# A retention and gated feed-forward kernel: the first two pair tiles taken from two batches in place of one

## The chip, the cores and the metric

The kernel runs on one core of a Trainium2 chip. The metric is the device time of one execution, in microseconds. The core has a matrix engine (TensorE, PE in the profile, with its weight loads as PEld), a vector engine (VectorE, DVE), a scalar engine (ScalarE, ACT), a general engine (GpSimd, POOL), an engine that issues transfers (SyncE, SP), and 16 DMA engines. Each engine works through its own instructions in order, and waits on semaphores for what other engines make.

## The reference

```python
B, H, S, D = 8, 8, 576, 64
scores = q @ k^T / sqrt(D)                       # per batch and head
gamma  = 1 - 2 ** (-5 - arange(H))
Dmat   = where(i >= j, gamma_h ** (i - j), 0)
attn   = (scores * Dmat) @ v                     # no softmax
x      = attn.transpose(0, 2, 1, 3).reshape(4608, 512)
gate   = sigmoid(x @ w_gate)                     # w_gate, w_val: 512 x 1536
out    = ((gate * (x @ w_val)) @ w_out)          # w_out: 1536 x 512
```

Inputs and output are float32. Since the decay is a product of a factor of the query's place and one of the key's, what a chunk of tokens owes to all earlier ones is q times a state, and the state is the sum of the outer products of k and v over those earlier tokens.

## The kernel before

**Tokens.** The 4608 columns of x are dealt out in an order of their own. The first 768 are three "pair tiles" of 256 tokens, listed in `PAIRS` (line 105) as (batch, which 256 tokens): the first 512 tokens of batch 0, then the first 256 tokens of batch 1. The rest goes in steps of 128 tokens (`STEPS`); the first two steps are chunks 2 and 3 of batch 1. Half a pair tile, called a = 0 or 1, is a chunk of 128 tokens with a place r = 0 or 1 inside each pair of neighbours.

**A pair tile.** q and k are cast to bfloat16 with their decay factors (`cast_pair`), turned on TensorE (`turn`, tiles kT and qT, copied by ACT), multiplied to scores (`pair_qk`, tiles qkp) and masked on DVE to ptp. Line 586 (`pair_intra`, for the third tile line 549 in `third_intra`) multiplies ptp with the values vp. The chunk's part from earlier chunks is line 596 (`pair_inter`), q times a state. The sum in tile pvp is copied to xT by ACT or DVE (`pair_out`, line 606).

**States before.** `first_st` (line 508) makes the outer products of the first two tiles into two PSUM banks, `tile_sv` and `first_sum` cast or add their useful quarters into `sbd`, three states in a row: after chunk 0, 1 and 2, and `sbd[3]` after all of batch 0's first 512 tokens. The third tile's state comes from `pair_st` (line 492). It needs for its second chunk only the state of its own first chunk (`third_inter`, into a bank `apart` that `third_out` adds). `first_batch_state` puts batch 0's last state in its final layout with two transfers and two copies on ACT.

**The hidden layer of the first 512 columns** is made in 12 blocks of 128 hidden units, each with a gate (hg, sigmoid on ACT) and a value (hv, multiplied on DVE into gv). Blocks 0 and 1 are made on 256 columns at a time by `h_half` (line 1344), the first half of them between the steps of the second tile; blocks 2 to 11 by `h_both` (line 1280) on 512 columns. Then `op_first` (line 1430) multiplies gv with w_out into three banks, op_0 to op_2, and later a fourth; the third tile's steps stand between these matmuls.

**What sets the order.** The order is written out by hand in the main body; every engine keeps the order of these calls. The weights come by the queue of SP in the order of the `load_w`, `load_wo` and `load_pair` calls, are cast by POOL, ACT or DVE as each `cast_w` or `cast_wo` names it, and a landing buffer is used again after its cast. `fill` puts idle matmuls on TensorE. `w_sums` makes sums of weight quarters on DVE for the later blocks (line 365; tiles wgt and wvt). Everything from the 768th column on is set by tables that the change leaves alone.

Of the kernel before, what the change touches and what calls it, by code (L numbers as in the profile page):

```python
# [16 lines left out]
def kernel(  # L17
# [19 lines left out]
    nc = tc.nc  # L37
# [67 lines left out]
    PAIRS = [(0, 0), (0, 1), (1, 0)]  # L105
# [107 lines left out]
    load_w(2, 2)  # L213
    load_w(4, 4)
    load_w(8, 4)
    pair_2 = load_pair(2)
    for n_wo, n_pair in ((2, 4), (4, 2), (6, 0)):
        for _ in range(n_wo):
            load_wo(sum(1 for x in parts if x[0] == "o"))
        for _ in range(n_pair):  # L220
            next(pair_2)
# [60 lines left out]
    sbd = [lead.tile([P, M, P], BF16, name="sbd0")]  # L282
    sbd += [sum_tile([P, 2, M, P], BF16, f"sbd{i}", SUMS - i)[:, 0] for i in range(1, 4)]
# [201 lines left out]
    def pair_st(A, a):  # L485
        b, a2 = PAIRS[A]
        if b not in st_tiles:
            st_tiles[b] = st_psum.tile([P, M, D], FP32, tag="st", name=f"st_{b}")
        for r in range(2):
            for m in range(M):  # L490
                for hh in range(2):
                    nc.tensor.matmul(st_tiles[b][half(hh), m, :], lhsT=natural["k", A][half(a), r, 2 * m + hh, :],
                                     rhs=natural["v", A][half(a), r, head(A, m, hh), :],
                                     start=(a2 == 0 and a == 0 and r == 0 and m == 0),
                                     stop=(a2 == 1 - b and a == 1 and r == 1 and m == M - 1),
                                     skip_group_check=True)

    def first_st(*tiles):


        for A, a in tiles:
            if (0, A) not in st_tiles:
                pool, tag = ((st_psum, "st"), (ffn_psum, "ffn"))[A]
                st_tiles[0, A] = pool.tile([P, M, P], FP32, tag=tag, name=f"st_0_{A}")
        for m in range(M):
            for r in range(2):
                for A, a in tiles:
                    nc.tensor.matmul(st_tiles[0, A][:, m, :],
                                     lhsT=natural["k", A][half(a), r, 2 * m:2 * m + 2, :],
                                     rhs=natural["v", A][half(a), r, 2 * m:2 * m + 2, :],  # L510
                                     start=(a == 0 and r == 0 and m == 0), stop=(a == 1 and r == 1 and m == M - 1),
                                     skip_group_check=True)

    def first_sum(sb, name, copy):

        share = nat_pool.tile([P, M, D], FP32, tag="s32", name=name, bufs=5)
        for hh in range(2):
            copy(out=share[half(hh)], in_=st_tiles[0, 1][half(hh), :, half(hh)])
        for hh in range(2):
            nc.vector.tensor_tensor(out=sb[half(hh), :, half(hh)], in0=st_tiles[0, 0][half(hh), :, half(hh)],  # L520
                                    in1=share[half(hh)], op=ALU.add)

    def tile_sv(A, a, engs):
        b, a2 = PAIRS[A]
        sb = sbd[2 * A + a]
        for hh in range(2):
            engs[hh](out=sb[half(hh), :, half(hh)], in_=st_tiles[b, 0][half(hh), :, half(hh)])
        state[b, 2 * a2 + a, 1] = sb
# [27 lines left out]
    def third_inter(bank):  # L556

        apart = bank[0].tile([P, 2, P], FP32, tag=bank[1], name="pvp_5_apart")
        for u in range(2):
            for y in range(2):  # L560
                for x in range(2):
                    nc.tensor.matmul(pair_ps[5][2 + u][0][half(x), 2 + u, :] if y else apart[half(x), u, :],
                                     lhsT=state[1, 0, 1][half(y), 2 * u + x, :],
                                     rhs=turned["qp", 2][half(y), 2 * u + x, P:2 * P],
                                     start=(y == 0 and u == 0), stop=(u == 1), skip_group_check=True)
        return apart

    def third_out(apart):

        ps = pair_ps[5][0][0]  # L570
        share = sum_tile([P, 2, 256], FP32, "apart", 4)[:, :, 0:P]
        nc.vector.tensor_copy(out=share, in_=apart)
        cols = slice(5 * P, 6 * P)
        nc.vector.tensor_tensor(out=x_out(slice(0, 2), cols), in0=x_in(ps[:, 0:2], cols), in1=x_in(share, cols), op=ALU.add)
        nc.scalar.copy(out=x_out(slice(2, 4), cols), in_=x_in(ps[:, 2:4], cols))
# [15 lines left out]
    def pair_inter(A, a):  # L591
        b, a2 = PAIRS[A]
        c = 2 * a2 + a
        for m in range(M):
            ps, at_m, of = pair_ps[2 * A + a][m]
            nc.tensor.matmul(ps[:, at_m, :], lhsT=state[b, c - 1, 1][:, m, :],
                             rhs=turned["qp", A][:, m, a * P:(a + 1) * P],
# [173 lines left out]

    def first_batch_state():

        whole = new_state((0, LAST - 1, NJ - 1))
# [520 lines left out]
    for A in range(2):  # L1295
        for g in range(2):
            cast_pair("v", A, g, on_pool)
# [267 lines left out]
```

## Time and profile before

| what | value |
|---|---|
| runs | 304.59, 305.26, 305.45 us |
| median | 305.26 us |
| span of the profiled execution | 304.6 us (the page gives no other time for it) |
| instructions | 10848 |
| granted TensorE clock, mean | 0.994 |
| HBM traffic | 37.75 MB read, 9.44 MB written |

Times in the profile's lists count from the span's start. A row of a timeline gives the start, the length and the engine and line, then the tile written and what it reads, the shape, and in brackets how long the engine sat idle ahead of it and on what. The chain of waits is followed back from the last instruction: at each step to what released it. A row of the windows gives one stretch: its length, then for each engine the busy time and number of instructions, then the granted clock, the busy share of the DMA engines and the GB/s they moved. TensorE's ends are modelled, and a few per cent of its records are missing.

### The profile page before, as it was taken

How to read it: one execution, taken by the hardware profiler on the slowest of the kernel's cores; microseconds unless marked ns; L12 is line 12 of the kernel's file. 1: busy time of each engine (PE TensorE's matmuls, PEld its weight loads, DVE VectorE, ACT ScalarE, POOL GpSimd, SP SyncE). 2: the span in 40 equal slices, each digit the busy share in tenths (PEclk: the TensorE clock that was granted, in tenths of full speed). 3: DMA queues.
4: the chain of work that ended last, by engine and by line, in shares of the span. 5: the costliest groups of instructions: out<-in, count | busy, mean ns of one | idle time of the engine just before them, and what ended most of it. 6: DMA issues, size and time to landing. Idle time of an engine off the chain costs nothing.

```text
span 304.6 us, 10848 instructions
## 1 busy us (share of the span) xinstructions
PE 296.0 (97%) x4427; PEld 244.8 (80%) x4436; DVE 244.7 (80%) x476; ACT 196.8 (65%) x420; POOL 208.6 (68%) x255
## 2 busy tenths in 40 slices
PE   8799999999999999999999999999999999999994
PEld 7674455877858888888888888888888888888883
DVE  6847997887997898689978997898789968946793
ACT  6646563526549656975796579657965886648640
POOL 5675653654557699769976997699769916751670
PEclk9989999999999999999999999999999999999999
DMA  7999999999999993999499919994980390012004
GB/s 214 328 346 399 360 296 230 186 215 199 204 209 238 194 240 82 242 264 213 110 210 234 213 44 219 225 203 52 214 199 2 100 245 9 2 56 87 1 2 138
DMA packets 144994, 55.01 MB, mean 181 GB/s; under 512 B 124336, under 2 KB 136880, under 8 KB 144944
## 3 DMA queue, kind: packets, MB, share of 16 engines
q1 hardware_dynamic: 144144, 53.66, 73.5%
q8 instruction: 35, 0.57, 0.8%
q10 hardware_dynamic: 800, 0.66, 0.7%
q14 instruction: 15, 0.12, 0.1%
HBM read 37.75 MB, written 9.44 MB: 155 GB/s over the span
## 4 chain that ended last, share of the span: by engine, by line
PE 92%; DMA 2%; SPq 2%; DVE 1%; issue 1%; POOL 0%
PE gatea L974 12%; PE wa L974 12%; PE qa L1088 11%; PE qe L1088 9%; PE gatee L974 6%; PE we L974 6%; PE h_v L850 4%; PE h_g L850 3%; PE op L1430 3%; PE op L1190 3%; PE gateg L974 3%; PE wg L974 3%; PE hv L1280 3%; PE hg L1280 3%; PE val L680 2%; DMA v32p<-in_v_dram 2%
## 5 line engine op out<-in xcount | busy, mean ns | idle before, releaser
L425 POOL TENSOR_TENSOR qk<-k,ktab 128x512 bf16<-128x512 f32 x30 | 32.4, 1080 | 11.8 <-DMA k<-in_k_dram 10.9
L1088 PEld LDWEIGHTS <-gsum 128*128 128x128 bf16 x336 | 31.9, 98 | 5.0 <-DVE gsum L911 0.8
L911 POOL TENSOR_TENSOR gsum<-gv 128x256 bf16<-128x256 bf16 (+1 forms) x35 | 26.5, 767 | 13.1 <-DVE gv L999 12.0
L974 PEld LDWEIGHTS <-wg_sb 128*128 128x128 bf16 x308 | 30.1, 98 | 3.7
L425 POOL TENSOR_TENSOR qk<-q,qtab 128x512 bf16<-128x512 f32 x28 | 30.8, 1100 | 3.3 <-DMA q<-in_q_dram 3.3
L974 PEld LDWEIGHTS <-wv_sb 128*128 128x128 bf16 x308 | 30.1, 98 | 3.5
L974 PEld LDWEIGHTS <-wvt 128*128 128x128 bf16 x280 | 27.4, 98 | 3.2
L974 PEld LDWEIGHTS <-wgt_sb 128*128 128x128 bf16 x252 | 24.7, 98 | 2.8
L999 POOL TENSOR_TENSOR gv<-gv,wu 128x512 bf16<-128x512 bf16 x7 | 8.1, 1161 | 25.6 <-DVE wu L1025 25.6
L1088 PEld LDWEIGHTS <-gv 128*128 128x128 bf16 x240 | 23.0, 98 | 3.0
L911 POOL TENSOR_TENSOR gsum<-gv,gsum 128x256 bf16<-128x256 bf16 x37 | 25.4, 715 | 0.0
L669 DVE TENSOR_TENSOR pt<-row,tri 128x256 bf16<-128x256 f32 x60 | 21.3, 414 | 4.4 <-PE row L662 3.7
L740 ACT CAST xT<-val 128x256 bf16<-128x256 f32 x60 | 18.9, 388 | 6.2 <-PE val L695 6.2
L974 PE MATMUL wa<-xsum,wv_sb 128*128 128x256 bf16 x140 | 21.0, 273 | 0.0
L631 ACT CAST sb<-s 128x256 bf16<-128x256 f32 x46 | 17.8, 417 | 3.7 <-DVE s L767 2.5
L974 PE MATMUL gatea<-xsum,wg_sb 128*128 128x256 bf16 x140 | 19.9, 273 | 0.0
L430 POOL CAST v<-v 128x512 bf16<-128x512 f32 x20 | 13.6, 681 | 8.7 <-DMA v<-in_v_dram 8.7
L999 POOL TENSOR_TENSOR gv<-gv,ws 128x512 bf16<-128x512 bf16 x15 | 17.4, 1163 | 2.8 <-DVE ws L1028 2.8
L1028 DVE TENSOR_TENSOR gs<-gatea,gs 128x512 f32<-128x512 f32 x21 | 13.9, 688 | 6.1 <-PE gatea L974 5.2
L1020 DVE TENSOR_TENSOR gatee<-gatea,gs 128x512 f32<-128x512 f32 x14 | 9.8, 700 | 10.0 <-PE gatea L974 7.2
L1028 DVE TENSOR_TENSOR ws<-wa,ws 128x512 f32<-128x512 f32 x21 | 14.4, 686 | 4.1 <-PE wa L974 4.1
L997 ACT ACTIVATE gv<-gs 128x512 bf16<-128x512 f32 x21 | 13.0, 631 | 7.0 <-DVE gs L1028 7.0
(181 smaller groups left out, 858.4 us busy)
## 6 DMA issues: line engine op xcount, KB each, us to landing
k<-in_k_dram SPq DMA_DIRECT2D x26, 256.0 KB, 4.5
q<-in_q_dram SPq DMA_DIRECT2D x26, 256.0 KB, 4.5
v<-in_v_dram SPq DMA_DIRECT2D x26, 256.0 KB, 4.2
out_dram<-ob SPq DMA_DIRECT2D x25, 256.0 KB, 3.2
wg<-in_moe_w_gate_dram SPq DMA_DIRECT2D x12, 256.0 KB, 5.3
wv<-in_moe_w_val_dram SPq DMA_DIRECT2D x12, 256.0 KB, 5.2
wo<-in_moe_w_out_dram SPq DMA_DIRECT2D x12, 256.0 KB, 5.1
v32p<-in_v_dram SPq DMA_DIRECT2D x6, 256.0 KB, 5.2
```

The lines of the kernel that those rows point to most:

```text
L425: eng.tensor_tensor(out=natural_qk[s][:, i].rearrange("p m (y d) -> p y m d", y=2), in0=by_halves(loaded[s][1 - i]), in1=tab, op=ALU.mult)
L430: eng(out=natural["v", s], in_=loaded[s][2])
L631: eng(out=state[key], in_=src)
L669: nc.vector.tensor_tensor(out=probs[s][:, y], in0=row_ps[s][y][:, 0], in1=tri.unsqueeze(1).to_broadcast([P, M, 64]), op=ALU.mult)
L740: nc.scalar.copy(out=x_out(ALL, cols_of(s, i)), in_=x_in(val_ps[s][i], cols_of(s, i)))
L850: nc.tensor.matmul(ps[:, i], lhsT=w_sb[:, kc, (fc + i) * P:(fc + i + 1) * P], rhs=xT(kc, slice(t0, t0 + n)), start=(kc == 0), stop=(kc == ...
L911: eng.tensor_tensor(out=to, in0=a, in1=b, op=op)
L974: nc.tensor.matmul(ps[:, f], lhsT=w[:, kc, f * P:(f + 1) * P], rhs=x[:, kc], start=(first and f == 0 and kc == 0), stop=(f == 1 and kc == ...
L999: eng.tensor_tensor(out=to, in0=to, in1=src, op=ALU.mult)
L1028: nc.vector.tensor_tensor(out=me["s5"], in0=a, in1=me["s5"], op=ALU.add)
L1088: nc.tensor.matmul(ps[:, b], lhsT=left(fp)[:, b * P:(b + 1) * P], rhs=right(fp), start=(first and fp == 0 and b == 0), stop=(fp == NFC // ...
L1280: nc.tensor.matmul(ps, lhsT=(wg_sb if what == "g" else wv_sb)[:, kc, fc * P:(fc + 1) * P], rhs=xT(kc, slice(0, 4 * P)), start=(kc == 0), s ...
```

## The change

`PAIRS` becomes tokens 0 to 255 of batch 0, tokens 0 to 255 of batch 1, tokens 256 to 511 of batch 0. So the first two tiles need only a state of their own first chunk each, and the third tile needs two states of the first batch. What goes with it:

- `first_st` makes the state of a tile's first chunk in two parts, one for each half of the heads; `first_state` casts it. `sbd` has two tiles in place of four. `first_sum`, `tile_sv`, `third_out` and `first_batch_state` go away.
- `pair_st` can take all 128 rows. It runs once for each of the first two tiles, between blocks 0 and 1, and gives the state after 256 tokens (`first`, and in bfloat16 `first_bf`). For the third tile it runs once for each half, in two banks. DVE adds the first half's state to `first`, ACT casts the sum, and `third_inter` multiplies q with both states, in two calls with a marker each.
- Blocks 0 and 1 are made on 512 columns by `h_one`, blocks 2 to 7 two at a time by `h_two`, half of the inner dimension at a time.
- The weights of blocks 4 to 7 are loaded 256 columns at a time; six tiles of w_out come ahead of the third tile's q and k in place of two. More of the value casts are ACT's. 16 idle matmuls fewer are put in.

```diff
-    PAIRS = [(0, 0), (0, 1), (1, 0)]
+    PAIRS = [(0, 0), (1, 0), (0, 1)]
...
-    load_w(2, 2)
-    load_w(4, 4)
+    for f in range(2, 8, 2):
+        load_w(f, 2)
...
-    for n_wo, n_pair in ((2, 4), (4, 2), (6, 0)):
+    for n_wo, n_pair in ((6, 4), (2, 2), (4, 0)):
...
+    def pair_st(A, a, bank):
+        rows_ = slice(0, P) if a is None else half(a)
+        st_tiles[A, a] = bank[0].tile([P, M, D], FP32, tag=bank[1], name=f"st_{A}_{a}")
...
+    def first_st(A, g, bank=None):
+        if g == 0:
+            st_tiles[A] = bank[0].tile([P, M, P], FP32, tag=bank[1], name=f"st_{A}")
+        for m in range(2 * g, 2 * g + 2):
+            for r in range(2):
+                nc.tensor.matmul(st_tiles[A][:, m, :], lhsT=natural["k", A][half(0), r, 2 * m:2 * m + 2, :],
+                                 rhs=natural["v", A][half(0), r, 2 * m:2 * m + 2, :],
+                                 start=(m == 0 and r == 0), stop=(m == M - 1 and r == 1), skip_group_check=True)
+
+    def first_state(A, engs):
+        for hh in range(2):
+            engs[hh](out=sbd[A][half(hh), :, half(hh)], in_=st_tiles[A][half(hh), :, half(hh)])
...
+    def third_inter(same):
+        for u in range(2):
+            for x in range(2):
+                for a in range(2):
+                    y = a if same else 1 - a
+                    kc = 2 * y + u
+                    nc.tensor.matmul(pair_ps[4 + a][kc][0][half(x), kc, :],
+                                     lhsT=state[0, 1 + a, 1][half(y), 2 * u + x, :],
+                                     rhs=turned["qp", 2][half(y), 2 * u + x, a * P:(a + 1) * P],
+                                     start=False, stop=(u == 1), skip_group_check=True)
...
+    def h_one(what, fc):
+        ps = pool.tile([P, 512], FP32, tag=tag, name=f"h{what}_0_{fc}")
+        for kc in range(NKC):
+            nc.tensor.matmul(ps, lhsT=(wg_sb if what == "g" else wv_sb)[:, kc, fc * P:(fc + 1) * P],
+                             rhs=xT(kc, slice(0, 4 * P)), start=(kc == 0), stop=(kc == NKC - 1))
...
-    fill(12)
+    fill(8)
...
-    first_st((0, 1), (1, 0))
-    tile_sv(0, 1, (on_act, on_act))
...
-    h_half("g", 0, 0, g0)
-    first_sum(sbd[2], "share_0", on_dve)
...
+    first_st(1, 0, FF[0])
+    pair_inter(0)
+    for a in range(2):
+        pair_tile(1, a, QK[a:a + 1])
+        pair_intra(1, 0, a)
+    first_st(1, 1)
+    first_state(1, (on_act, on_dve))
+    pair_out(0, 1, on_act)
+    pair_intra(1, 1, 0)
+    pair_out(1, 0, on_dve)
+    pair_intra(1, 1, 1)
+    pair_inter(1)
+    pair_out(1, 1, on_act)
+    h_one("g", 0)
+    h_one("v", 0)
+    pair_st(0, None, ST)
+    h_one("g", 1)
+    pair_st(1, None, TR)
+    h_one("v", 1)
...
+    pair_st(2, 0, ST)
+    op_first((7,), range(3), opps)
+    pair_st(2, 1, TR)
+    op_first((8, 9), range(3), opps)
+    casts_to(0)
+    running[0] = new_state((0, 2, 1), FP32)
+    nc.vector.tensor_tensor(out=running[0], in0=first[:, 0], in1=st_tiles[2, 0], op=ALU.add)
+    keep_state((0, 2, 1), running[0], on_act)
...
+    third_intra([PV, QK[0]])
+    third_inter(True)
+    mark(*ST)
+    op_first((10,), range(3), opps)
+    mark(*ST)
+    third_inter(False)
+    pair_out(2, 0, on_act)
+    pair_out(2, 1, on_act)
```

**Three places in the order.** On ACT, from the first state cast to the first sigmoids, there stood before (sbd: a state, xT: columns of x, gv: a hidden block, pvp_0: a chunk's attention, its number telling which chunk):

```order
L527 CAST sbd_290<-st_0_486 64x4x64 x2
L606 CAST xT_534<-pvp_0_517 128x4x128
L606 CAST xT_534<-pvp_0_536 128x4x128
L527 CAST sbd_291<-st_0_486 64x4x64 x2
L1350 ACTIVATE gv_0_621<-hg_611 128x256
L606 CAST xT_534<-pvp_0_578 128x4x128
L1350 ACTIVATE gv_0_621<-hg_647 128x256
```

The same place on ACT now:

```order
L510 CAST sbd_290<-st_466 64x4x64 x2
L510 CAST sbd_291<-st_533 64x4x64
L577 CAST xT_514<-pvp_0_516 128x4x128
L577 CAST xT_514<-pvp_0_551 128x4x128
L1263 ACTIVATE gv_0_594<-hg_0_589 128x512
L1263 ACTIVATE gv_0_594<-hg_1_619 128x512
L308 CAST wv_sb<-wv_2_1_139 128x2x256
```

The sigmoid of 256 columns that stood ahead of the last copy to xT is gone; all copies to xT stand ahead of the first sigmoid, which is of 512 columns.

On DVE, at the end of the hidden layer's first 512 columns, there stood before (qp: the third tile's q, gv: hidden blocks, wvt: weight sums):

```order
L412 TENSOR_TENSOR qp_793<-q32p_0_179,qtab_255 128x4x2x64
L1285 TENSOR_TENSOR gv_2_795<-gv_2_795,hv_8_823 128x512
L1285 TENSOR_TENSOR gv_2_795<-gv_2_795,hv_9_829 128x512
L412 TENSOR_TENSOR qp_793<-q32p_1_183,qtab_255 128x4x2x64
L1285 TENSOR_TENSOR gv_2_795<-gv_2_795,hv_10_836 128x512
L1285 TENSOR_TENSOR gv_2_795<-gv_2_795,hv_11_842 128x512
L365 TENSOR_TENSOR wvt_862<-wv_sb 128x512
```

The same place on DVE now:

```order
L1247 TENSOR_TENSOR gv_2_756<-gv_2_756,hv_8_789 128x512
L1247 TENSOR_TENSOR gv_2_756<-gv_2_756,hv_9_795 128x512
L1247 TENSOR_TENSOR gv_2_756<-gv_2_756,hv_10_801 128x512
L411 TENSOR_TENSOR qp_807<-q32p_0_187,qtab_255 128x4x2x64
L1247 TENSOR_TENSOR gv_2_756<-gv_2_756,hv_11_809 128x512
L411 TENSOR_TENSOR qp_807<-q32p_1_191,qtab_255 128x4x2x64
L364 TENSOR_TENSOR wvt_830<-wv_sb 128x512
```

Both casts of the third tile's q moved two or three products later, the second one behind the last product of the group.

On DVE, at the third tile, there stood before (ptp: the last masked scores, qk and v: the first step's q and values, apart and xT: the third tile's output, s: a running state, ob: an output row):

```order
L478 TENSOR_TENSOR ptp_1_946<-qkp_1_1_950,trip 128x512
L425 TENSOR_TENSOR qk_1003<-q_0_850,qtab_276 128x2x4x64
L430 CAST v_1006<-v_0_852 128x512
L572 COPY apart<-pvp_apart 128x2x128
L574 TENSOR_TENSOR xT_1067<-pvp_0_1009,apart 128x2x128
L1464 COPY s_1_1_1_1073<-st_969 128x256
L882 COPY ob_1083<-op_0_873 128x512
```

The same place on DVE now:

```order
L477 TENSOR_TENSOR ptp_1_916<-qkp_1_1_920,trip 128x512
L424 TENSOR_TENSOR qk_985<-q_0_818,qtab_276 128x2x4x64
L429 CAST v_988<-v_0_820 128x512
L1442 TENSOR_TENSOR s_0_2_1_990<-first,st_0_942 128x256
L1445 TENSOR_TENSOR sf_3_1_994<-s_0_2_1_990,st_1_962 128x256
L844 COPY ob_1061<-op_0_835 128x512
```

Two sums of states stand where the third tile's output stood; the first of them feeds the state that the third tile's second chunk is multiplied with, so that it stands ahead of that chunk's products and no longer behind them.

257 lines of the change are left out of this document (99 added, 158 removed).

## The prediction

> **What bounds the kernel now.** I read the page first (busy shares, clock), then the list of waits of PE, then the chain of waits from 6 us on, then single engines around the places that the change touches.
>
> ```profile
> PE 296.0 (97%) x4427; PEld 244.8 (80%) x4436; DVE 244.7 (80%) x476; ACT 196.8 (65%) x420; POOL 208.6 (68%) x255
> PE st L508 <- POOL vp L409: 1.3, 1, 1.3
> PE qkp L471 <- ACT qT L462: 0.3, 2, 0.2
> 50.50:289.00 238.50, 237.62 (x3782) 205.09 (x3785) 196.23 (x372) 164.67 (x360) 172.54 (x196) 1.00 0.74 160
> ```
>
> TensorE is the bound. After the start it waits for anything worth naming once, 1.3 us, for the cast of the first batch's values. From 50.5 us to 289 us it is busy 237.6 of 238.5 us, and the instructions there are the same before and after. So whatever TensorE gains or loses before about 50 us should arrive at the end undiminished, and only that part has to be costed. The chain of that part (start, length, what):
>
> ```profile
> 6.91 5.80 DMA v32p<-in_v_dram
> 12.76 0.63 POOL vp L409
> 13.42 0.38 PE st L508 x4
> 13.80 0.35 PE qkp L471 x16
> 14.15 0.81 PE pvp L586 x32
> 14.97 0.54 PE pvp L596 x4
> 15.51 0.97 PE st L508 x11
> 16.48 1.02 PE pvp L586 x32
> 17.49 0.81 PE hg L1344 x4
> 18.30 0.22 PE pvp L596 x4
> 18.53 0.55 PE st L508 x8
> 22.55 0.21 PE hg L1280
> 36.36 3.45 PE hv L1280 x16
> 39.81 0.22 PE op L1430
> 44.51 0.25 PE st L492 x16
> 48.10 0.57 PE pvp L549 x32
> 49.20 2.11 PE op L1430 x9
> ```
>
> Three marks: 13.42, when the values are cast; 22.55, when the gate of column block 2 begins; 39.81, when the output product begins. From the second to the third both kernels run the same 80 matmuls of 512 columns.
>
> ```profile
> 14.60:18.00 3.40, 3.40 (x65) 2.52 (x60) 2.25 (x6) 1.91 (x4) 2.72 (x6) 0.50 0.99 307
> ```
>
> Between 14.6 and 18.0 us the granted clock is 0.50. That is why 32 matmuls of line 586 take 1.02 us there and 0.81 us just ahead, and four of line 596 take 0.54 us against 0.22 us later.
>
> **Edit 1: the first two tiles.** The values still land at the same place in the queue, so 13.42 stays. Four groups of idle matmuls lose 16 matmuls in all; I cost this at nothing, since behind two of the groups TensorE waits for ACT anyway (the 0.3 us above), and the rest ends in the wait for the values. If that cover were gone, it could only gain. The second tile's last scores (16 of line 471, 0.35 us) now run inside that wait. From 13.42, with the dip of the clock kept, TensorE does: 4 state matmuls 0.38, 32 of line 586 0.81, 4 state matmuls 0.24 (a quarter of 0.97, which the chain gives for 16 of which it has 11 records), the first tile's 4 of line 596 0.54, 16 of line 586 0.51, 4 state matmuls 0.24. That ends at 16.14. Then comes a serial piece:
>
> ```profile
> 12.76 1.88 POOL L409 CAST vp<-v32p 128x512 bf16<-128x512 f32 x3 [1.39 <-DMA v32p<-in_v_dram]
> 13.84 0.75 ACT L527 CAST sbd<-st 64x256 bf16<-64x256 f32 x2 [1.58 <-PE st L508]
> 14.90 0.61 PE L596 MATMUL pvp<-qT,sbd 128*128 128x128 bf16 x4
> 15.54 0.59 ACT L606 CAST xT<-pvp 128x512 bf16<-128x512 f32 x1 [0.33 <-PE pvp L596]
> 19.46 0.39 PE L596 MATMUL pvp<-qT,sbd 128*128 128x128 bf16 x4
> 19.88 0.59 ACT L606 CAST xT<-pvp 128x512 bf16<-128x512 f32 x1 [1.15 <-PE pvp L596]
> ```
>
> The second tile's values are cast by 14.64 (12.76 + 1.88), so they are not late. Its state is cast on two engines, 0.38 each, while TensorE does the last 16 of line 586 (0.51, to 16.65). Line 596 then takes 0.64 until ACT starts (14.90 to 15.54), the copy 0.59, the handover 0.05: the first hidden matmul starts at 17.93. Before, this copy (19.88) was hidden by hidden-layer matmuls on the first 256 columns; those now need all 512, so the copy stands on the path. Behind that copy on ACT nothing else is late.
>
> Then 16 matmuls of 512 columns at 0.216 (3.45 / 16) make 3.45 us, and two new state products come in between. Such a product (16 matmuls, all 128 rows, 64 weights each) is not in the trace. Below, it costs 0.25 (line 492, same count, four quarters of the array at once), above 1.10 (line 508: 0.55 for 8, times two). I take 0.50: half arrays, two at once in place of four. So block 2 begins at 17.93 + 3.45 + 1.00 = 22.38 against 22.55, **0.17 us earlier**. The bounds: with the clock at full speed the same sum gives 17.25 for the first hidden matmul (state matmuls 0.27 a group, line 596 0.22 and 0.42, 16 of line 586 0.40), so 21.2 at the least and 23.6 at the most: from 1.35 earlier to 1.05 later.
>
> **Edit 2: the weights' order and casts.** Blocks 4 to 7 come in eight loads of 256 columns in place of eight of 512, and more value casts go to ACT.
>
> ```profile
> 28.62 0.60 ACT L1283 ACTIVATE gv<-hg 128x512 bf16<-128x512 f32 x1 [0.27 <-PE hg L1280]
> 29.98 1.13 ACT L309 CAST wg_sb<-wg 128x512 bf16<-128x512 f32 x2
> 18.00:20.00 2.00, 2.00 (x26) 1.68 (x24) 1.29 (x3) 0.51 (x2) 1.58 (x5) 1.00 0.96 329
> 26.00:28.00 2.00, 2.00 (x11) 0.89 (x10) 1.90 (x4) 0.84 (x2) 0.88 (x2) 1.00 1.06 398
> ```
>
> Block 8's gate weights are cast by 31.1, and its matmuls start near 32.9 (36.36 - 3.45); the two casts on ACT now follow block 7's sigmoid, which ends near 31.6 (22.38, five pairs of blocks of 1.73, 0.60), and end near 32.7; the matmuls need the second and the fourth quarter only 0.2 and 0.6 after their start. Cost nothing. If the small rows ran at the 329 GB/s of 18 to 20 us in place of 398, their 2.1 MB would cost 1.1 us more of queue; below, nothing. I take nothing: TensorE trails these loads by a microsecond or more.
>
> **Edit 3: the third tile.** It now belongs to the first batch and needs two earlier states, the second of which is made from its own first half: a sum on DVE, a cast on ACT, then the products.
>
> ```profile
> 36.39 1.11 DVE L412 TENSOR_TENSOR qp<-q32p,qtab 128x512 bf16<-128x512 f32 x1
> 38.80 0.68 DVE L412 TENSOR_TENSOR qp<-q32p,qtab 128x512 bf16<-128x512 f32 x1
> 39.40 1.28 DVE L1285 TENSOR_TENSOR gv<-gv,hv 128x512 bf16<-128x512 bf16 x2
> 40.59 0.76 DVE L365 TENSOR_TENSOR wvt<-wv_sb 128x512 bf16<-128x512 bf16 x1
> 42.13 0.43 DVE L365 TENSOR_TENSOR wvt<-wv_sb,wvt 128x512 bf16<-128x512 bf16 x1
> 47.61 0.43 DVE L430 CAST v<-v 128x512 bf16<-128x512 f32 x1 [0.19 <-DMA v<-in_v_dram]
> 49.91 0.41 DVE L1464 COPY s<-st 128x256 f32<-128x256 f32 x1
> 44.80 0.37 ACT L631 CAST sb<-st 128x256 bf16<-128x256 f32 x1
> ```
>
> Call T the start of the output product. TensorE reaches the products with the states after 30 output matmuls (6.48), 4 groups of transposes (0.22 each before, 0.88), scores 0.57, two state products 0.50, line 549's 0.57: T + 9.0. DVE: before, the six weight sums start at 40.59 (T + 0.78) and the cast of v ends at 48.04, with 0.19 of waiting in it, 7.26 us of work. Now both casts of q stand behind the tenth and the eleventh product of the last group, so the sums start later: product 10 ends near T, cast 0.6 to 1.0, product 11 0.6, cast 0.6 to 1.0, that is T + 1.8 to 2.6. Then 7.26 of the same work, the sum 0.41, the cast on ACT 0.37, handovers 0.1: the state is there at T + 9.9 to 10.7. **TensorE waits 0.9 to 1.7 us**; if the three slow weight sums (0.76 against 0.43) ran fast as well, none. I take 1.0, near the short end, because the later of the two casts quoted, the one beside the end of this stage, took 0.68. Queued behind the waiting product are the last six output matmuls of the three rows. Nothing covers this: they come behind it in order.
>
> Beside it, the third tile has 8 more small products (before, 8 and 16 small ones took 0.53 between 48.67, where line 549 ends, and 49.20), 0.2 here, and two markers of two tiny matmuls, 0.1. Moving a state product ahead is neutral. From T to the last six output matmuls: before 49.20 - 39.81 = 9.39; now 9.0 + 1.0 + 0.5 (16 products, 0.4, with markers 0.1) = 10.5, **1.1 later**; 0.1 without the wait, 1.9 at the upper end of it. The two small DMA issues and two ACT copies that built the first batch's last state go away; they are not on the chain, and gain nothing.
>
> **The sum.** -0.17 + 0 + 1.1 = +0.9 on a span of 304.6 us, which is the only time that the page gives for the profiled execution; the runs have a median of 305.26 and a lowest of 304.59, so the profile sits at their low end. I add a tenth for the handovers that I rounded off (five of about 0.04): +1.0, **306.3 us** against the median.
>
> **The rivals.**
> (a) The state is in time. DVE works through its sums at 0.43 each and the products of the last states never wait. Place: the third tile; price: the 1.0 us; it decides if the cast of v ends on DVE before T + 8.1. For it: DVE sat idle 1 us after that cast before. Against: three of six sums took over 0.7 us. Then -0.17 + 0.1 + 0.1, 305.3 us, not slower; with the clock kept as in (b) too, about 304.6.
> (b) The clock is not halved. The wait for the values is now cut in two by 16 score matmuls, so the stretch before 14.6 has more work in it. Then block 2 begins 0.85 earlier (17.25 in place of 17.93 and 0.17): -0.85 + 1.2, 305.6 us. Against: 16 filling matmuls are gone.
> (c) The clock is halved one stretch later. TensorE now idles about 0.7 us for the copy at the end of the stretch 14.6 to 18.0, having waited for a state too. Then the first hidden matmuls run at half speed for 3.4 us and lose 1.7: -0.85 + 1.7 + 1.2, 307.3 us.
> (d) The weight rows of 256 columns delay the queue by up to 1.1 us, so the step loads behind them land late and DVE's cast of v, and with it the state, comes 0.6 later: 306.9 us.
> The Trainium skill, "TensorE: Matmul & The Clock Gate", section "Why this matters for your kernels", says that the clock drops after gaps of more than about 3 us. By that rule (b) would hold, as neither kernel has such a gap; the trace does not agree, as the clock fell to 0.50 behind a gap of 1.3 us.
>
> **How the numbers follow.** Forecast 0.45, (a) 0.20, (b) 0.12, (c) 0.15, (d) 0.08. Within 0.3% (0.9 us), about what a measurement of this kernel can tell from no change: a quarter of the forecast's cases, whose size lies close to that bound, half of (a), most of (b), in all 0.28. Faster: the other half of (a), where the clock is kept or a state product costs 0.25, and a little of (b), 0.12. Slower: 0.60, the rest of the forecast, (c) and (d). The likeliest case alone reaches from 305.7 to 307.6 (wait 0.9 to 1.7, state products 0.35 to 0.8 each). The range, 304.3 to 308.0, goes down to (a) with a kept clock and up past (c).
>
> **What would show it.** Right: TensorE waits near 48.5 to 50 us for ACT's cast of the state, about 1 us; ACT's second copy of the second tile ends just ahead of the first hidden matmul, at 17.9; block 2 begins within 0.3 us of 22.4; a clock of 0.50 from 14.6 to 18.0. Wrong: no wait in the third tile (a); a clock of 1.00 throughout (b), or of 0.50 from 18 to 21.4 (c); waits for weights between 22 and 40 us (d); or a loss behind 50 us, which I hold to be only a shift.

## The result and the profile after

| | median, us | executions | difference to the kernel before run beside it |
|---|---|---|---|
| before | 305.03 | 6, 304.07 to 306.27 | |
| changed | 309.04 | 6, 307.93 to 309.86 | +4.01, ratio 1.0125 [1.0089, 1.0162] |

The change makes the kernel slower, as forecast, but by four times the forecast 1.0 us, and the time lies above the forecast range. The ratio and its 95% interval are worked out from the single executions, so they differ a little from the quotient of the medians.

The times are device times. In the executions shown here the device time was 1.7 to 1.9 us above the span (309.05 and 307.2 for the profile of the changed kernel; two of e14 below had 2.0 and 2.4). So the execution of the kernel before that the prediction was read from, with a span of 304.6 us, took about 306.4 us if the same difference holds: just above every one of the six executions in the table. The half clock in it is not typical either, as the first experiment and the count behind e12 show.

The page of the changed kernel has for the busy times (engine, us, share, instructions):

```profile
PE 297.0 (97%) x4428; PEld 242.5 (79%) x4428; DVE 242.4 (79%) x467; ACT 195.2 (64%) x414; POOL 209.4 (68%) x255
```

TensorE is the bound as before, 1 us busier and waiting more. Its windows, for the stretch in which the clock was halved before and for the long rest (length, then PE, PEld, DVE, ACT and POOL, the granted clock, DMA share and GB/s):

```profile
14.60:18.00 3.40, 2.17 (x49) 1.53 (x49) 1.91 (x4) 1.43 (x3) 2.13 (x4) 1.00 0.95 265
...
55.00:289.00 234.00, 233.87 (x3749) 202.00 (x3748) 193.66 (x366) 161.59 (x353) 168.64 (x192) 1.00 0.73 158
```

Here the clock stays at 1.00, but between 14.6 and 18.0 us TensorE is busy for 2.17 of 3.40 us only, where it was busy throughout before. From 55 us on it is busy all the time again, so the loss lies ahead of that. PE's list of waits up to 62 us names what it waits for (total, times, longest):

```profile
PE qkp L470 <- ACT qT L461: 1.1, 3, 0.6
...
PE op L1409 <- DVE gv L1247: 0.8, 1, 0.8
PE hg L1259 <- ACT xT L577: 0.7, 1, 0.7
PE pvp L568 <- DVE sbd L510: 0.6, 1, 0.6
PE pvp L545 <- ACT sb L602: 0.5, 1, 0.5
```

The chain of waits puts the four last of these in their places (start, length, what):

```profile
14.52 0.38 PE st L503 x4
...
15.60 0.34 PE st L503 x4
...
15.96 0.37 ACT sbd L510
...
16.84 0.41 PE pvp L568 x4
...
17.28 0.59 ACT xT L577
...
17.91 1.02 PE hg L1259 x4
...
19.80 0.37 PE st_None L491 x16
...
22.48 1.73 PE hg L1274 x8
...
40.93 1.02 PE op L1409 x4
...
50.46 0.41 ACT sb L602
...
50.92 0.28 PE pvp L545 x5
...
53.88 0.45 PE turn L587 x8
...
56.05 0.87 PE h_g L812 x8
```

The chain goes by way of the casts there, and so leaves out what TensorE does beside them. TensorE's timeline has it:

```profile
15.85 0.44 PE L559 MATMUL pvp<-ptp,vp 64*64 64x128 bf16 x16
16.84 0.40 PE L568 MATMUL pvp<-qT,sbd 128*128 128x128 bf16 x4 [0.55 <-DVE sbd L510]
17.91 1.02 PE L1259 MATMUL hg<-xT,wg_sb 128*128 128x512 bf16 x4 [0.68 <-ACT xT L577]
```

Of the 1.97 us between the last state matmul (end 15.94) and the first hidden matmul (17.91) TensorE is busy for 0.75 and stands bare for 0.55 and 0.68, together 1.23. At the start of the output product it waits for a product on DVE, and in the third tile for the cast of the state. The timeline of DVE, in the same form, shows that the two halves of the second state's cast were not made side by side, as DVE's waited for ACT's, and what holds up the output product:

```profile
16.36 0.43 DVE L510 CAST sbd<-st 64x256 bf16<-64x256 f32 x1 [0.97 <-ACT sbd L510]
...
39.60 0.68 DVE L411 TENSOR_TENSOR qp<-q32p,qtab 128x512 bf16<-128x512 f32 x1
40.20 0.68 DVE L1247 TENSOR_TENSOR gv<-gv,hv 128x512 bf16<-128x512 bf16 x1
40.80 0.68 DVE L411 TENSOR_TENSOR qp<-q32p,qtab 128x512 bf16<-128x512 f32 x1
```

The third row of output needs the bank that the last hidden block still holds. Its product on DVE (40.20) stands behind a cast of the third tile's q (39.60), so TensorE, done with the hidden layer at 39.75 (80 matmuls and 17.27 us behind 22.48), does the two output matmuls that need no other bank and gets going at 40.93 only, after a wait of 0.75 us.

### The profile page after: what moved, and what is told of

Read it like the earlier page. It is cut to its first block, busy times and chain, and to the rows that moved or that the text cites. A ratio compares the mean times of both kernels' runs of the same rounds, so it can differ in the third digit from the quotient of the medians.

```text
span 307.2 us, 10825 instructions
## 1 busy us (share of the span) xinstructions
PE 297.0 (97%) x4428; PEld 242.5 (79%) x4428; DVE 242.4 (79%) x467; ACT 195.2 (64%) x414; POOL 209.4 (68%) x255
## 4 chain that ended last, share of the span: by engine, by line
PE 89%; DVE 4%; SPq 2%; DMA 2%; issue 1%; ACT 1%; POOL 0%; DVEq 0%
PE gatea L936 12%; PE wa L936 12%; PE qa L1050 11%; PE qe L1050 9%; PE gatee L936 6%; PE we L936 6%; PE h_v L812 3%; PE h_g L812 3%; PE op L1152 3%; PE wg L936 3%; PE gateg L936 3%; PE op L1409 3%; SPq L184 2%; PE val L651 2%; DMA v32p<-in_v_dram 2%; PE hv L1274 2%
```

## The experiments

Differences are to the kernel before, run beside each kernel on the same chip (its medians: 304.92, 304.85, 304.89, 304.84 and 305.25 us in the five batches).

| kernel | median, us | difference | ratio and interval |
|---|---|---|---|
| e0, before again | 304.71 | -0.21 | 0.9989 [0.9970, 1.0009] |
| e1, output order | 309.18 | +4.26 | 1.0139 [1.0112, 1.0166] |
| e2, state sum first | 308.65 | +3.73 | 1.0117 [1.0089, 1.0145] |
| e3, both | 309.46 | +4.54 | 1.0142 [1.0110, 1.0175] |
| e4, block 0 in halves | 307.76 | +2.91 | 1.0126 [1.0080, 1.0171] |
| e5, q early | 307.67 | +2.82 | 1.0102 [1.0068, 1.0136] |
| e6, e2 + e4 + e5 | 306.39 | +1.54 | 1.0067 [1.0043, 1.0091] |
| e7, before with q late | 306.91 | +2.06 | 1.0064 [1.0036, 1.0093] |
| e8, idle matmuls back | 307.71 | +2.82 | 1.0091 [1.0072, 1.0110] |
| e9, e6 + e8 | 306.24 | +1.35 | 1.0045 [1.0027, 1.0063] |
| e10, e9 without two products | 306.08 | +1.19 | 1.0048 [1.0020, 1.0076] |
| e11, before with fewer idle | 305.55 | +0.71 | 1.0024 [0.9997, 1.0051] |
| e12, changed again | 308.93 | +4.09 | 1.0133 [1.0099, 1.0168] |
| e13, e8 again | 308.57 | +3.73 | 1.0121 [1.0085, 1.0157] |
| e14, changed, no idle | 315.28 | +10.03 | 1.0342 [1.0297, 1.0386] |
| e15, before, no idle | 308.83 | +3.58 | 1.0102 [1.0050, 1.0154] |

**e0: the kernel before, as it is.**

> The kernel before, unchanged, run again to see its profiled execution. Theory A (the loss of 4.0 us is in waits that the trace after shows: 0.8 for a PSUM bank at the start of the output product, 0.7 and 0.6 at the second tile, 0.5 for the third tile's state, and 0.7 of added state products): this execution too has a half clock from about 14.6 to 18 us and a span near 304.6. Rival B (the profiled execution of before was one of its slow ones: the changed kernel's time lies 1.85 us above its span, 309.05 against 307.2, and by the same rule a span of 304.6 belongs to a time of 306.4, above the median): spans of 302.5 to 304 in most executions, a clock of 1.00 from 14.6 to 18 us, and about 1.0 to 1.3 of the 4.0 us are explained by which execution was profiled.

Twelve executions took 303.83 to 305.94 us. The profiled one (304.42 us, span 302.7) has no half clock. Its window:

```profile
14.60:18.00 3.40, 3.40 (x69) 2.75 (x64) 2.80 (x6) 1.60 (x5) 2.34 (x4) 1.00 1.03 312
```

Its chain, at the marks of the prediction:

```profile
14.42 0.38 PE st L508 x7
...
15.40 0.54 PE hg L1344 x4
...
20.19 1.73 PE hg L1280 x8
...
37.45 0.21 PE op L1430
...
48.95 0.45 PE turn L616 x8
...
51.12 0.87 PE h_g L850 x8
```

Rival B holds, and this is the comparison that the prediction should have had. In this execution block 2 begins at 20.19, not at 22.55: the clock is full, the casts of the first tile's values end at 11.95 where the recorded one began the second of them at 12.76, hidden matmuls on the first 256 columns run from 15.40 on between the state casts and the copies, and TensorE waits for none of them. Against it the changed kernel is 2.29 us later at block 2 (22.48), 2.30 at the end of the hidden layer (39.75 against 37.45), and 4.93 at the turn and at the first h_g (53.88 and 56.05 against 48.95 and 51.12). The span differs by 4.5. One execution is not the usual one by itself: this one lies 0.3 us under the median of the twelve, and in the profile of e7 below, a kernel whose start is that of the kernel before, the values came late again, without a halved clock (TensorE waits 1.5 us for them), and block 2 began at 21.64.

**e1, e2, e3: the two waits of the second half.** e1 gives the output product its old start, so that its third row comes later; e2 puts the third tile's state sum ahead of the casts that it waited behind; e3 does both.

```diff
-    op_first((0, 1), range(3), opps)
+    op_first((0,), (0,), opps)
     turn("k", 2, 0, *TR)
-    op_first((2,), range(3), opps)
+    op_first((1,), (0,), opps)
     turn("q", 2, 0, *PV)
-    op_first((3,), range(3), opps)
+    op_first((0, 1), (1,), opps)
     turn("k", 2, 1, *QK[0])
-    op_first((4,), range(3), opps)
+    op_first((0, 1), (2,), opps)
     turn("q", 2, 1, *QK[0])
+    op_first((2, 3, 4), range(3), opps)
...
-    casts_to(0)
     running[0] = new_state((0, 2, 1), FP32)
     nc.vector.tensor_tensor(out=running[0], in0=first[:, 0], in1=st_tiles[2, 0], op=ALU.add)
     keep_state((0, 2, 1), running[0], on_act)
+    casts_to(0)
```

> The changed kernel with the first matmuls of the output product in the order of the kernel before (two into the first bank, with the transposes between, then the second bank, then the third). Theory A: the wait of 0.8 us for the third bank goes, but DVE's weight sums end no earlier, so the scores of the third tile wait less and the state is late by 0.4 more: 0.4 to 0.6 us faster than the changed kernel, 308.5. Rival (waits here only move, the third tile's state sets the time): within 0.2 us of the changed kernel, 309.0, with a wait of 1.3 us or more at the third tile. Rival B has no say.

> The changed kernel with the sum of the third tile's state and its cast ahead of the first step's casts on DVE. Theory A: the state is there 1.6 us earlier (0.6 for q, 1.2 for v less the handover), TensorE does not wait for it: 0.5 to 0.7 us faster than the changed kernel, 308.4. Rival (the casts of the first step, now later, make TensorE wait at the turning of step 0 or in the steps behind): no gain, 309.0, with a new wait at line 587.

> Both edits in one. Theory A: the two waits no longer trade against each other: 1.3 to 1.6 us faster than the changed kernel, 307.6. Rival (the third tile is bound by the masks on DVE, which begin when the weight sums end): 0.7 faster at most, 308.3, with a wait of TensorE for ptp at line 531.

e1 gains nothing, as its rival had it. The wait for the bank is gone, and its list of waits names what came in its place:

```profile
PE qTp L451 <- DVE qp L411: 1.5, 1, 1.5
```

In its chain, that place:

```profile
39.21 0.24 PE kTp L451 x4
39.44 0.68 DVE gv L1247
40.12 0.97 DVE qp L411
...
41.14 0.40 PE qTp L451 x4
```

With the old start the first turn of q comes 0.4 us behind the start of the output product, and it needs both casts of q (the third tile's heads are interleaved, so a turn reads pairs from both), the second of which now stands behind the last product. The wait only moved. e2 shows no wait for the state and gains about 0.3 us against the +4.01 of the changed kernel, which is within the scatter. And its profile doesn't show that the edit removed the wait, since it comes and goes by itself. Of the six profiled executions that have this place as the changed kernel has it (its own, e4, e8, e12, e13 and e14, the later ones described below) four have it, 0.4 to 0.7 us, and e4 and e12 have none. What differs is how long the casts ahead of the sum took on DVE, here in the changed kernel's first profile and in that of e12:

```profile
48.83 1.27 DVE L429 CAST v<-v 128x512 bf16<-128x512 f32 x1
...
50.51 0.42 DVE L429 CAST v<-v 128x512 bf16<-128x512 f32 x1
```

Why the same cast took 1.27 or 0.42 us stays open. Both expectations for e3 missed: it adds nothing to e2, and TensorE waits for no ptp; its profiled execution had the clock halved behind the second tile.

**e4: something to put between.** Block 0 of the hidden layer on 256 columns again.

```diff
+    h_part("g", 0, 0, g0)
     pair_inter(1)
     pair_out(1, 1, on_act)
-    h_one("g", 0)
-    h_one("v", 0)
     pair_st(0, None, ST)
+    h_part("v", 0, 0, v0)
+    h_part("g", 0, 1, g0)
+    h_part("v", 0, 1, v0)
     h_one("g", 1)
```

> Changed kernel, with block 0 of the hidden layer made on 256 columns at a time again: the first tile's half of its gate stands ahead of the second tile's products with the state, the rest behind the first new state product. Theory A (the second tile's state cast and the copy behind it stand bare on TensorE's path, 0.9 and 0.66 us in the chain of the changed kernel, because nothing is left to put between): about 1.0 us of the 1.56 is covered, 0.6 to 1.2 us faster than the changed kernel, so 307.8 to 308.4 us, with block 2 at 21.3 to 21.9 us in place of 22.48. Rival B (what comes behind waits for weights or casts anyway, so the gain is eaten by block 4 or by the output product): 308.9 to 309.2.

The 0.9 and 0.66 us of the expectation are read from the chain, which leaves out the matmuls of line 559; TensorE's idle time is 1.23. e4 gains 1.1 us against the changed kernel (+2.91 in place of +4.01), though its interval is wide, since one of its five executions took 310.75 us at a clock of 0.988. The chain of its profiled execution:

```profile
15.09 0.34 PE st L503 x4
...
16.35 0.60 PE hg L1345 x4
...
21.46 1.73 PE hg L1274 x8
```

From the start of the last state matmuls to block 2 it takes 6.37 us (15.09 to 21.46) in place of 6.88 (15.60 to 22.48), and TensorE's idle time there is 0.71 in place of 1.23, so 0.5 us of the gain is cover. Where the rest comes from stays open. It is not only that fewer executions have a halved clock (counted below): without those under a mean clock of 0.995 the medians are 307.53 us (4 executions) and 308.89 (7 of the changed kernel, with e12).

**e5: the third tile's q early.**

```diff
-    for n_wo, n_pair in ((6, 4), (2, 2), (4, 0)):
+    for n_wo, n_pair in ((2, 4), (4, 2), (6, 0)):
...
     cast_wo(0, on_pool)
+    cast_pair("k", 2, 0, nc.gpsimd)
+    cast_pair("k", 2, 1, nc.gpsimd)
     step(units, 2)
...
     step(units, 2)
+    cast_pair("q", 2, 0, nc.vector)
+    step(units, 2)
...
+    cast_pair("q", 2, 1, nc.vector)
+    step(units, 2)
...
```

The start of the output product is e1's.

> Changed kernel, with the third tile's q and k loaded behind two rows of the output weights in place of six, their casts as early in the order as in the kernel before, and the old start of the output product (the same start as in e1, where the third tile's q came too late for it). Theory A (the late q is the one cause behind the bank wait of 0.8 to 1.3 us, behind the 1.5 us wait that took its place in e1, and behind the late state of the third tile, since both casts stand between the last products on DVE): all three go, 1.3 to 2.0 us faster than the changed kernel, 307.0 to 307.7 us; TensorE waits at no place from 22 to 55 us for more than 0.5. Rival B (DVE has too much to do there and the wait moves once more): 308.6 to 309.3.

e5 and e1 differ in where the third tile's rows stand among the loads and the casts of the output weights (some of which change between POOL and ACT with it), and by 1.44 us (+2.82 against +4.26); the median lies at the upper end of theory A. Between 22 and 55 us no wait above 0.2 us is left. Its chain at the marks:

```profile
22.01 1.73 PE hg L1274 x8
...
39.28 0.21 PE op L1409
...
51.69 0.45 PE turn L587 x8
```

From the start of the output product to the turn it takes 12.41 us; the changed kernel took 14.13 (39.75 to 53.88), and the kernel before 11.50 (37.45 to 48.95). TensorE is idle for 1.33 us of the 14.13 and for nothing of the other two. So 1.72 us of the changed kernel's stage are gone in e5, 1.33 of them waiting, and the 0.91 that are left against the kernel before are work: two state products of 0.37 in place of 0.25 and about 0.2, more small products, markers.

**e6: e2, e4 and e5 together.**

> The edits of e2 (the third tile's state sum ahead of the first step's casts on DVE), e4 and e5 together on the changed kernel. Theory A (the loss sits in two places that do not touch each other): the gains add up, 0.4 + 0.6 to 1.2 + 1.3 to 2.0, 305.5 to 306.7 us; what is left against the kernel before is the two state products (0.74 us) and the part of the copy that stays bare. Rival B (the three share one bottleneck): not better than the best of them, 307 us or more.

+1.54 us. The single gains, 0.28, 1.10 and 1.19 against the changed kernel, add up to 2.57, and 2.47 is what was found, as theory A had it. So the losses look separate, as far as intervals of 0.7 us and more to either side can tell.

**e7: the late q alone, in the kernel before.** The load order and the late casts of the change, everything else as before.

```diff
-    for n_wo, n_pair in ((2, 4), (4, 2), (6, 0)):
+    for n_wo, n_pair in ((6, 4), (2, 2), (4, 0)):
...
-    cast_pair("k", 2, 0, nc.gpsimd)
-    cast_pair("k", 2, 1, nc.gpsimd)
     cast_wo(1, on_dve)
-    cast_pair("q", 2, 0, nc.vector)
     units = h_both((8, 9, 10, 11))
...
+    cast_wo(5, on_act)
+    cast_pair("k", 2, 0, nc.gpsimd)
+    cast_pair("k", 2, 1, nc.gpsimd)
+    step(units, 3)
+    cast_pair("q", 2, 0, nc.vector)
+    step(units, 1)
     cast_pair("q", 2, 1, nc.vector)
-    step(units, 2)
```

> The kernel before, with one thing of the change: the third tile's q and k are loaded behind six rows of the output weights in place of two, and cast late, the second cast of q behind the last product of the hidden layer. Pairs, states and the hidden layer as before. Theory A (these moves, which the prediction costed at nothing as loads and only through DVE as casts, cost as much by themselves): a wait of TensorE for q's cast near 38 us, 1.2 to 2.0 us slower than the kernel before, 306.1 to 306.9 us. Rival B (the loss comes with the new states and batches alone): 304.6 to 305.2 us.

+2.06 us, just above the expected 1.2 to 2.0, without any of the new states. Loads and casts moved together here, so the run doesn't tell one from the other. In its list of waits:

```profile
PE qTp L452 <- DVE qp L412: 1.1, 1, 1.1
```

The loads stand ahead of these casts. The DMA issues of q's tiles in e0 (shortest, median and longest duration in ns, then the first and the last start in us):

```profile
L184 SPq DMA_DIRECT2D q32p<-in_q_dram x6: 379/532/950, 1.3 to 29.1; - x6
```

The same in the changed kernel:

```profile
L184 SPq DMA_DIRECT2D q32p<-in_q_dram x6: 379/572/692, 1.3 to 33.1; - x6
```

The last of them is issued 4.0 us later, behind four more rows of the output weights. In e0 the first of the two casts waits for its load already:

```profile
33.87 0.95 DVE L412 TENSOR_TENSOR qp<-q32p,qtab 128x512 bf16<-128x512 f32 x1 [0.75 <-DMA q32p<-in_q_dram]
```

So this cast at least could not have stayed where it was.

**e8, e9, e10: idle matmuls and state products.** e8 puts the 16 idle matmuls back into the changed kernel, e9 into e6; e10 is e9 without the two new state products (the later chunks of the first two batches then lack what they owe to the first 256 tokens).

```diff
-    fill(8)
+    fill(12)
...
-    fill(4)
-    turn("q", 0, 1, *PV)
     fill(8)
+    turn("q", 0, 1, *PV)
+    fill(12)
...
-    fill(4)
+    fill(8)
     turn("k", 1, 1, *TR)
...
-    pair_st(0, None, ST)
...
-    pair_st(1, None, TR)
...
-        nc.vector.tensor_copy(out=first[:, b], in_=st_tiles[b, None])
+        nc.vector.memset(first[:, b], 0.0)
```

> Changed kernel with the 16 idle matmuls put back (groups of 12, 8, 12 and 8 where the kernel before has them). So far 2 of 6 executions of the changed kernel, and 10 of 39 of it and its variants, had a mean clock of 0.988 to 0.994 and took 1 us or more longer; none of 40 of the kernel before had. Theory A (the gaps that the idle matmuls filled are what lets the clock fall in some executions): no execution under 0.995, the others as before, median 308.3 to 308.9 us. Rival B (the new bare waits at the second tile, 0.9 and 0.66 us, let it fall, and they are still there): 2 or 3 of 8 executions under 0.995, median 308.8 to 309.4. If the prediction's reading was wrong that they lie in waits anyway, the start moves later by up to 16 x 0.06 = 0.9 us and the median is 309.5 or more.

> e6 with the 16 idle matmuls back. Theory A (no bare wait above 0.7 us is left at the second tile, and e6 had no execution under 0.995, so nothing is left for them to hold up): 306.2 to 306.6, as e6. Rival B (the 1.1 us that TensorE waits in e6 for the turned q ahead of the scores is idle time that they would fill, and the start comes no later): same time too, but the clock never under 0.999. Rival C (they are work on the path): 306.9 or more.

> e9 with the two state products over all 128 rows of the first two tiles left out (the states after 256 tokens are then zero, so every later chunk of these two batches lacks what it owes to them). Theory A (what is left of the loss after e6 is work: these two products, 0.37 us each bare on TensorE's path): 0.6 to 0.9 us faster than e9, 305.4 to 305.9 us, still not under the kernel before. Rival B (the rest lies in the third tile or in the start, and something else would wait in their place): within 0.3 us of e9.

e8 came out below both expectations, with no execution under a mean clock of 0.995; e9 lies 0.15 us under e6, as its theory A had it. e10 missed its theory A and came out within the 0.3 us of its rival B: without the two products the way from the last state matmuls to block 2 is 0.82 us shorter (15.99 to 21.56 in place of 15.81 to 22.20), yet the median is 0.16 us lower only. In its profiled execution TensorE waits 1.29 us at 68.9 us for nothing that the profile shows, in the middle of an output product where e9 has no such wait. It is also the slowest of the nine, 1.85 us above their median. One execution doesn't say whether that is the rule, so where the 0.8 us went stays open.

**e11 to e15: what the idle matmuls are worth.** e11 takes 16 out of the kernel before (8, 4, 8 and 4 in place of 12, 8, 12 and 8), e12 and e13 are the changed kernel and e8 side by side, e14 and e15 have none of these groups at all.

> The kernel before with 16 idle matmuls fewer (8, 4, 8 and 4 in place of 12, 8, 12 and 8), nothing else. Theory A (they are not filling: without them TensorE's first gaps let the clock fall in some executions, or the start ends later): 305.6 to 306.2 us, or executions under 0.995. Rival B (the prediction's step: they lie in waits anyway): 304.6 to 305.2 us and no execution under 0.995.

> The changed kernel as it is, on one chip with e11 and e13. Theory A: 308.7 to 309.3 us, as on record, with some executions under 0.995. Rival B (e8 differed from it by the chip alone): 307.6 to 308.2, as e8.

> The kernel of e8. Theory A: 307.5 to 308.1 us and 0.8 to 1.4 below e12. Rival B: within 0.4 us of e12.

> Changed kernel with the four groups of idle matmuls at the start gone altogether (24 fewer than it has). Theory A (each idle matmul that goes costs about 0.04 us or lets the clock fall more often): 309.6 to 310.2 us, or more than half of the executions under 0.995. Rival B (they lie in waits anyway and the differences so far are scatter): 308.6 to 309.3.

> The kernel before without its 40 idle matmuls at the start. Theory A: 306.2 to 306.9 us, more than twice the +0.7 of e11. Rival B: 304.5 to 305.3.

e12 came out as on record, and e13 lies 0.36 us under it, as its rival B had it, but e8, the same kernel as e13 on the same chip, lay 0.86 under e13. All executions together, the changed kernel has a median of 309.03 (11) and that with 16 more idle matmuls 308.37 (12). e11 gives +0.7 with nought just inside its interval, and two of its twelve executions under 0.995. So the 16 are worth 0 to 1 us, probably about 0.7; the runs don't settle it. Without any, rival B fell twice, and theory A held in kind, not in size: all six executions of e14 and five of the six of e15 are under 0.995, but e14 loses 6.0 us against the changed kernel and e15 2.9 more than e11 (2.3 without its execution of 313.41 us, which the ratio leaves out), far more than the matmuls would in proportion. The windows of e14:

```profile
4.60:8.00 3.40, 1.70 (x35) 1.22 (x32) 1.39 (x2) 1.93 (x4) 1.19 (x2) 0.98 1.09 316
8.00:24.90 16.90, 14.70 (x183) 9.03 (x180) 8.57 (x15) 6.63 (x12) 12.65 (x21) 0.50 1.06 335
```

Half busy ahead of 8 us, and then 16.9 us at a clock of 0.50. So these matmuls keep the clock up, and the number that is left decides steeply.

e12 caught the changed kernel itself with the clock halved. Its windows:

```profile
14.60:18.00 3.40, 2.18 (x51) 1.53 (x50) 2.22 (x4) 1.43 (x3) 2.55 (x5) 1.00 1.05 310
18.00:21.40 3.40, 3.40 (x10) 1.03 (x11) 0.00 (x0) 0.60 (x1) 2.52 (x8) 0.52 1.06 365
```

Its chain there:

```profile
17.96 1.74 PE hg L1259 x4
19.70 1.71 PE hv L1259 x4
```

The hidden matmuls behind the second tile's bare waits take 1.74 and 1.71 in place of 1.02 and 0.86. TensorE had been busy 2.18 of the 3.40 us ahead of them, against 2.17 in the first profile of the changed kernel, where the clock stayed up. So gaps of the same size are followed by this in some executions and not in others. Counted by the mean clock of each execution, where it is on record (one stretch of 3.4 us at half clock takes 0.0056 off the mean, so under 0.995 means about one such stretch or more): 4 of 83 of the kernel before; 13 of 45 of the kernels that have the second tile as changed and 24 or more idle matmuls (changed, e1, e2, e3, e5, e8, e12, e13); 1 of 27 of those with block 0 in halves (e4, e6, e9, e10). Those of the changed kernel took 309.7 to 310.8 us, the others 307.9 to 309.1.

No version with the change ran faster than the kernel before; the best of those that compute everything, e9, is 1.35 us slower.

## Why the prediction was wrong in size

**"Should arrive at the end undiminished": nearly right.** 4.93 us at the first h_g, 4.5 on the span.

**Edit 1, the mechanism: right; the sum: wrong, and this is the largest failure.** The changed kernel did what the steps said: first hidden matmul at 17.91 (forecast 17.93), block 2 at 22.48 (22.38). That these agree is partly luck: the clock was not halved, the second tile's values came later than assumed, the state products took 0.37 in place of 0.50, and the two casts of the second state ran one after the other (the row of 16.36) where I had them side by side. But the step compared this with a block 2 at 22.55, read from an execution in which the first tile's values came late and the clock was halved, "with the dip of the clock kept". In e0 it begins at 20.19. So against e0 the -0.17 should have been +2.3. From the last wait for values to block 2 it takes 7.96 us (14.52 to 22.48) in place of 5.77 (14.42 to 20.19): 1.23 are the bare waits, of which the forecast had only the second, for the copy (0.64); and 0.96 are more work, 0.74 of it the two state products. (The two marks are not quite the same: e0 waits there for the second half of the second tile's values, the changed kernel for the first half.) e0 took 0.6 us less than the median of 305.03, so against a median execution the miss here is probably smaller by as much; that is an estimate.

**The anchor.** "The only time that the page gives" was a span; I set it beside the medians of device times and concluded that the profile sat at their low end, when it sat about 1.1 us above the median (306.4 against 305.26). A sum of differences made against that execution, added to a median, hid the loss of edit 1.

**Rivals (a), (b) and (c): all seen, in different executions.** In e12 and e4 the third tile's state is in time, as (a) has it. The clock is kept in about seven of ten executions of these kernels (32 of 45); in the profiled ones in which it fell (e3, e12 and e13) it was halved one stretch later, behind the second tile's waits. Each was priced on the same wrong anchor, so no price was right. Nothing of (d) shows: TensorE waits for no weights behind 22.48, and DVE's casts at the third tile wait for no load. The sentence on the Trainium skill, "TensorE: Matmul & The Clock Gate", section "Why this matters for your kernels" (gaps of more than about 3 us drop the clock), does not hold in e14 either, whose clock fell at 8 us behind single waits of at most 0.84 us since the first matmul. The same page, section "What's actually happening", speaks of an activity window of 3413 ns that runs free of the kernel; this would fit the traces, as 2.17 and 2.18 us of work in the same 3.40 us were followed by a clock of 1.00 and of 0.52, but no run here shows where such a window begins.

**The idle matmuls "at nothing ... it could only gain": wrong in kind.** They were judged by the time that they take, and not by what they do for the clock. What the 16 cost is not settled (0 to 1 us); that the groups matter is (e14, e15).

**Edit 2, "cost nothing": right for the hidden layer's weights, whose matmuls ran without a wait** from 22.48 to the end of the hidden layer.

**Edit 3: one wait right in place, one missed.** The wait for the third tile's state came where forecast, 0.4 to 0.7 us in place of 1.0, in four of six profiled executions. But the step counted the two late casts of q only for what stands behind them on DVE. It did not ask what TensorE needs of the two things they are interleaved with: the bank held by the last product (0.75 us), or, with the other order, q itself (1.5). Nor did it ask why the casts had been moved: the q tiles are loaded 4 us later. e7 shows that late loads and casts together cost 2 us by themselves. And without the wait the step came to 0.1 us more where 0.91 of work was found. From the start of the output product to the turn it became +2.63 in place of +1.1.

Together, in the two profiled executions: +2.30 at the end of the hidden layer and +2.63 to the turn make +4.93, of which 4.5 reach the end. The medians differ by 4.0.

**Two slips of arithmetic** change nothing of this: the wait of 1.7 us would make the third tile 1.8 later, not 1.9, and the rest of the forecast with (c) and (d) is 0.57, not 0.60.

## What to carry to other kernels

Before you add differences to a median, find out whether the execution you read is a usual one: compare its device time, not its span, with the other times, and treat a halved clock in it as an accident that both kernels may or may not have. Where a change takes small independent work out from between casts and copies, count every handover that then stands bare. When a cast or load moves, ask of each instruction that it now stands ahead of whose bank or operand it frees.

## What the runs showed that was not expected

Leaving out the idle matmuls of the start costs the kernel before 1.0% (e15), and the changed one 6.0 of 309 us (e14): the clock stayed at 0.50 for 16.9 us, although TensorE was listed busy for 14.70 of them. In the first profile of the kernel before, the 3.40 us at half clock were listed as fully busy, and the clock then rose. In e14 the same stretch was listed as fully busy too, and the clock stayed at 0.50 behind it:

```profile
14.60:18.00 3.40, 3.40 (x60) 2.50 (x58) 1.98 (x4) 0.73 (x2) 2.45 (x4) 0.50 1.05 333
18.00:21.40 3.40, 2.40 (x30) 1.46 (x27) 1.12 (x2) 1.43 (x3) 2.72 (x7) 0.50 1.02 324
```

So the busy share of the profile alone does not tell when it comes back; what does was not tried.
